# A@V on 64x32 tiles of TensorE in place of 64x64, in a fused attention and MLP kernel

## The chip, the cores and the metric

The kernel runs on one NeuronCore of a Trainium2 chip. The core has five engines that work side by side, each through its own list of instructions in order: TensorE (PE in the profile; its weight loads are listed apart as PEld), VectorE (DVE), ScalarE (ACT), GpSimd (POOL) and SyncE (SP). They wait for each other through semaphores. TensorE multiplies a stationary operand (the weights, loaded first) with a moving operand that is streamed through, and writes to PSUM, a memory of eight banks; VectorE and ScalarE read PSUM. The metric is the time in microseconds (us) from launch to end on the device.

TensorE's array of 128 rows by 128 columns can be used as smaller tiles. A matmul that contracts over 64 rows and gives 64 output features takes a tile of 64x64, and four of them fit side by side; one with 32 output features takes a tile of 64x32, and eight fit. Which tile a matmul uses follows from the partitions at which its operands and its output begin. Matmuls on different tiles can run at the same time.

## The reference

```python
def _attn_ref(q, k, v):                      # q, k, v: 8 x 12 x 448 x 64, float32
    scores = scale * np.matmul(q, k.transpose(0, 1, 3, 2))
    attn = np.maximum(scores, 0.0) ** 2 / S
    return np.matmul(attn, v)

x = attn_out.transpose(0, 2, 1, 3).reshape(B * S, H * D)     # 3584 x 768
h = x @ w_in                                                 # 768 x 2048
g = np.maximum(h, 0.0) + alpha * np.minimum(h, 0.0)
out = g @ w_out                                              # 2048 x 768
```

There is no softmax: the scores go through a ReLU and are squared. "A@V" below is the product of these squares with v.

## The kernel before

The 96 heads (8 batches of 12) are taken in 24 quads of four heads, three quads a batch. Within a quad, a head is addressed by r (which half of the 128 partitions holds its 64 features of q and k, or its 64 keys) and s or c (which 64 of 128 output partitions it fills). The 448 positions of a head are cut into NJ = 7 parts of 64.

Scores. `chunk` takes the next of 24 x 7 parts: `score_mm` multiplies the 64 keys of part j with all 448 queries, for four heads, into a pair of PSUM banks (one bank per r), and `relu` takes the pair out to `rl` on ScalarE (L237) or VectorE (L239). `square` makes `at` from it (L248 or L250). For quads 0 to 4 (`n <= PE_TURNED`) q and k were turned by TensorE, and a chunk is four matmuls on 64x64 tiles (L221). For quads 5 to 23 they were turned by VectorE's 32x32 transposes and DMAs (`turn_dma`, L202 and L208). There the keys of a part lie in two blocks of 32, so a chunk is eight matmuls of 32 keys on 64x32 tiles (L229), all with 448 moving columns.

A@V. `attnv(n)` multiplies, for one quad, the seven `at` tiles with v. For each part j there are four matmuls (r and s), each with 64 keys to contract, 64 features of v as the weights and the 448 queries as the moving operand. They accumulate over j in one pair of banks, r choosing the bank and s the half of the partitions. Then the pair is scaled and copied to `xT`, one bank by ScalarE (L272) and one by VectorE (L274), or both by one of them.

The MLP. `f1_mm` (L294) computes h from `xT` on the full 128x128 array, six matmuls a part; `f1_out` makes g (`gT`) with one ScalarE (L300) and one VectorE (L301) instruction. The output product is computed for blocks of 128 rows, either directly (`f2`, L319) or for pairs of blocks with seven half-size products in place of eight (`Pair`: TensorE L354, sums on VectorE L350 and L359, copies on ScalarE L370 and L375), with weights mixed beforehand (`weight_mix`, L332). These too use the full array.

Order. Nothing is scheduled by a tool: `tc.manual_schedule()` is on, and the plan strings passed to `walk` spell out the order of all work, word by word: `cADA` is three (here A, D, A) chunks with the engine of their ReLU, `s0D` a square, `v` an A@V, `f` one part of the first MLP product, `p..` and `r..` products of a pair, `g..` a direct block, `n` the turning of the next quad with the loads that follow it. Each engine executes its instructions in that order, so an instruction that waits holds up all that is behind it on its engine. An A@V is mostly placed between chunks of a later quad. PSUM banks are handed out least recently used first (`take_pair` for chunks and A@V, `take_bank` for the MLP), and a matmul into a bank waits until what was in it has been read.

The lines that matter here: L260 (A@V's matmul), L229 and L221 (scores), L294, L319 and L354 (MLP), and, as what TensorE waits for, L237, L239, L272, L274, L321, L359 and L375.

Of the kernel before, what the change touches and what calls it, by code (L numbers as in the profile page):

```python
# [16 lines left out]
NJ = 7  # L17
PE_TURNED = 4
# [3 lines left out]
def kernel(  # L22
# [10 lines left out]
    nc = tc.nc  # L33
    B, H, S, D = q.shape
# [46 lines left out]
    def take_pair():  # L81
        lo = min((0, 2, 4, 6), key=lambda i: (max(taken[i], taken[i + 1]), i))
        take(lo, 2)
        return psum[:, lo:lo + 2]
# [168 lines left out]
    def attnv(n, eng="AD"):  # L253
        ps = take_pair()
        vv = vraw.pop(n)
        for j in range(NJ):
            a = att.pop((n, j))
            for r in range(2):
                for s in range(2):
                    nc.tensor.matmul(ps[64 * s:64 * s + 64, r, :S],  # L260
                                     vv[64 * r:64 * r + 64, s, j, :],
                                     a[64 * r:64 * r + 64, s],
                                     start=(j == 0), stop=(j == NJ - 1))
        b, g = divmod(n, NG)
        if g == 0:
            xT[b] = xT_pool.tile([128, NG, 2, S], BF16, tag="xT", name="xT")
        if eng == "A":
            nc.scalar.activation(xT[b][:, g], ps[:, :, :S], ACTF.Copy, scale=out_scale)
            return
        for r in range(2):  # L270
            if eng[r] == "A":
                nc.scalar.activation(xT[b][:, g, r], ps[:, r, :S], ACTF.Copy, scale=out_scale)  # L272
            else:
                nc.vector.tensor_scalar(xT[b][:, g, r], ps[:, r, :S], out_scale, None, ALU.mult)  # L274
# [164 lines left out]
    class Walk:  # L439
# [12 lines left out]
        def step(self, w):  # L452
# [6 lines left out]
            elif c == "v":  # L459
                if turn["v"] < NQ:  # L460
                    attnv(turn["v"], rest or "AD")
                    turn["v"] += 1
# [108 lines left out]
```

## Time and profile before

| | |
|---|---|
| median of 3 runs | 395.19 us (394.13 to 396.29) |
| profiled execution | 394.87 us, of which the span of instructions is 393.1 us |
| granted TensorE clock, mean | 0.991 |
| TensorE busy | 372.5 us, 95% of the span, 3633 matmuls in the records |
| A@V matmuls (L260) | 672 (24 quads x 28), 36.6 us busy |
| scores on 64x32 tiles (L229) | 1064 (19 quads x 56), 38.0 us busy |
| scores on 64x64 tiles (L221) | 140 (5 quads x 28) |
| VectorE, ScalarE busy | 304.9 us (78%), 258.8 us (66%) |

A line of a group names the source line, the engine, the operation, the tiles it writes and reads, for matmuls the rows and columns of the array that it uses (64*32), the moving operand's shape and the number of instructions. A matmul's duration goes from its start to its modelled end; since the next matmuls start well before that end, what a run of matmuls costs is read from its start to the start of what follows. In a listing in order of time the first number is the start, counted from the start of the span, and the second the length. What stands in square brackets is the idle time of the engine before it, with what ended it.

### The profile page before, as it was taken

What the parts mean: (1) busy time and instruction counts of PE and PEld (TensorE: products, weight loads), DVE (VectorE), ACT (ScalarE), POOL (GpSimd) and SP (SyncE); (2) the same over time, 40 slices, a digit from 0 to 9 for tenths busy, and PEclk for the clock granted to TensorE, in tenths of its full rate; (3) what the DMA queues carried; (4) which work ended last, traced back from release to release, by engine and by line L of the source; (5) the groups of instructions that cost most, each with busy time, mean ns of one, the idle gap of its engine ahead of it and who ended that gap; (6) DMA issues with size and microseconds to landing.
All of it is one profiled execution on the core that took longest, in us unless ns stands there. A gap on an engine that the chain in (4) does not pass through costs nothing.

```text
span 393.1 us, 9204 instructions
## 1 busy us (share of the span) xinstructions
PE 372.5 (95%) x3633; PEld 195.9 (50%) x3637; DVE 304.9 (78%) x467; ACT 258.8 (66%) x384; POOL 86.4 (22%) x140
## 2 busy tenths in 40 slices
PE   8899999499989998999989999899999999999996
PEld 6454555144444454545545455445555555555563
DVE  4988988655996989867788886888969875865753
ACT  5987674456766656768668676786587785874400
POOL 8566563500330323011220311303000000000000
PEclk9999999889999999999999999999999999999999
DMA  9999999952677755726766257664333321220024
GB/s 148 191 203 202 207 209 206 223 109 47 100 147 152 117 95 79 166 42 116 136 109 140 43 97 141 108 144 66 76 62 81 76 49 26 64 65 9 2 51 110
DMA packets 51676, 43.38 MB, mean 110 GB/s; under 512 B 8753, under 2 KB 51121, under 8 KB 51633
## 3 DMA queue, kind: packets, MB, share of 16 engines
q0 software_dynamic: 27744, 22.59, 40.0%
q1 hardware_dynamic: 23216, 19.62, 19.6%
q8 instruction: 28, 0.46, 0.5%
q10 hardware_dynamic: 672, 0.59, 0.4%
q14 instruction: 16, 0.12, 0.1%
HBM read 45.62 MB, written 11.01 MB: 144 GB/s over the span
## 4 chain that ended last, share of the span: by engine, by line
PE 72%; DVE 12%; SPq 6%; DMA 4%; issue 3%; ACT 1%; DVEq 0%; ACTq 0%
PE psum L294 30%; PE psum L354 24%; PE psum L260 7%; PE psum L229 6%; SPq L208 5%; DVE perm L202 3%; DVE at L250 3%; DMA T<-perm 2%; PE psum L319 2%; DVE gT L301 2%; DMA T<-w_mix 1%; DVE S L350 1%; PE psum L171 1%; DVE rl L239 1%; PE psum L221 1%
## 5 line engine op out<-in xcount | busy, mean ns | idle before, releaser
L294 PE MATMUL psum<-xT,w_in_sb 128*128 128x448 bf16 x768 | 152.6, 356 | 0.4 <-DVE gT L301 0.4
L237 ACT ACTIVATE rl<-psum 128x896 bf16<-128x896 f32 x128 | 111.4, 929 | 25.9 <-PE psum L229 23.4
L301 DVE SCALAR_TENSOR_TENSOR gT<-neg,beta_sb,psum 128x448 bf16<-128x448 f32 x128 | 84.0, 675 | 36.1 <-ACT neg L300 34.9
L294 PEld LDWEIGHTS <-w_in_sb 128*128 128x128 bf16 x768 | 74.2, 99 | 75.0 <-issue 9.7
L300 ACT ACTIVATE neg<-psum 128x448 f32<-128x448 f32 x128 | 68.9, 546 | 55.3 <-PE psum L294 39.6
L250 DVE TENSOR_TENSOR at<-rl 128x896 bf16<-128x896 bf16 x105 | 62.1, 617 | 3.8 <-ACT rl L237 3.7
L248 ACT ACTIVATE at<-rl 128x896 bf16<-128x896 bf16 x63 | 58.3, 951 | 1.5 <-DVE rl L239 1.2
L123 POOL DMA_DIRECT2D qraw<-in_q_dram x38 | 22.6, 600 | 137.3 <-DVE perm L202 129.8
L354 PEld LDWEIGHTS <-S 128*128 128x128 bf16 x384 | 36.4, 98 | 32.7 <-issue 10.0
L239 DVE TENSOR_SCALAR rl<-psum 128x896 bf16<-128x896 f32 x40 | 43.2, 1086 | 9.3 <-PE psum L229 8.1
L354 PE MATMUL psum<-w_mix,S 128*128 128x384 bf16 x288 | 49.9, 326 | 0.0
L229 PE MATMUL psum<-T 64*32 64x448 bf16 x1064 | 38.0, 358 | 7.1 <-DMA T<-perm 5.4
L354 PEld LDWEIGHTS <-gT 128*128 128x128 bf16 x296 | 28.3, 98 | 20.2 <-issue 1.8
L260 PE MATMUL psum<-at,vraw 64*64 64x448 bf16 x672 | 36.6, 352 | 0.0
L354 PE MATMUL psum<-w_out_sb,gT 128*128 128x384 bf16 x192 | 34.0, 326 | 0.0
L130 POOL DMA_DIRECT2D vraw<-in_v_dram x24 | 17.7, 739 | 51.7 <-PE psum L260 49.7
L229 PEld LDWEIGHTS <-T 64*32 64x32 bf16 x1064 | 12.7, 90 | 29.3 <-issue 26.9
L260 PEld LDWEIGHTS <-vraw 64*64 64x64 bf16 x672 | 19.4, 106 | 14.7 <-issue 6.5
L359 DVE TENSOR_TENSOR osb<-psum,u 128x384 f32<-128x384 f32 (+2 forms) x37 | 19.7, 542 | 9.0 <-PE psum L354 8.4
L123 POOL DMA_DIRECT2D kraw<-in_k_dram x38 | 22.9, 614 | 3.3 <-DMA vraw<-in_v_dram 1.4
L319 PE MATMUL psum<-w_out_sb,gT 128*128 128x256 bf16 (+1 forms) x124 | 22.5, 325 | 0.9 <-DVE gT L301 0.5
L274 DVE TENSOR_SCALAR xT<-psum 128x448 bf16<-128x448 f32 x24 | 14.9, 623 | 10.0 <-PE psum L260 9.9
(46 smaller groups left out, 240.2 us busy)
## 6 DMA issues: line engine op xcount, KB each, us to landing
out_dram<-osb SPq DMA_DIRECT2D x91, 96.0 KB, 2.2
T<-perm SPq DMA_DIRECT2D x128, 56.0 KB, 3.6
vraw<-in_v_dram POOLq DMA_DIRECT2D x24, 224.0 KB, 6.1
qraw<-in_q_dram POOLq DMA_DIRECT2D x38, 112.0 KB, 3.3
kraw<-in_k_dram POOLq DMA_DIRECT2D x38, 112.0 KB, 4.7
w_in_sb<-in_moe_w_in_dram POOLq DMA_DIRECT2D x16, 192.0 KB, 8.2
w_out_sb<-in_moe_w_out_dram POOLq DMA_DIRECT2D x4, 512.0 KB, 10.4
T<-w_mix SPq DMA_DIRECT2D x24, 56.0 KB, 5.3
```

The source lines that it names most:

```text
L123: nc.gpsimd.dma_start(out=t[64 * m:64 * m + 64].rearrange("p w j d -> p w (j d)"), in_=flat[2 * g + m])
L229: nc.tensor.matmul(ps[lo:lo + 32, r, :S], t[64 * r:64 * r + 64, 1, a, NJ * c + j], moving, start=True, stop=True)
L237: nc.scalar.activation(rl, ps[:, :, :S], ACTF.Relu)
L239: nc.vector.tensor_scalar(rl, ps[:, :, :S], 0.0, None, ALU.max)
L248: nc.scalar.activation(a, rl, ACTF.Square)
L250: nc.vector.tensor_tensor(a, rl, rl, ALU.mult)
L260: nc.tensor.matmul(ps[64 * s:64 * s + 64, r, :S], vv[64 * r:64 * r + 64, s, j, :], a[64 * r:64 * r + 64, s], start=(j == 0), stop=(j == NJ ...
L294: nc.tensor.matmul(ps, w_in_sb[:, km // 2, km % 2, bass.ts(ff, 128)], xT[b][:, km // 2, km % 2, :], start=(km == 0), stop=(km == KM - 1))
L300: nc.scalar.activation(neg, ps, ACTF.Relu, scale=-1.0)
L301: nc.vector.scalar_tensor_tensor(gT[:, ff, (b % 2) * S:(b % 2) * S + S], neg, beta_sb[:, ff:ff + 1], ps, ALU.mult, ALU.add)
L319: nc.tensor.matmul(ps, gT[:, ff, bass.ts(c, 128)], w_out_sb[:, ff, first_col + lo:first_col + hi], start=(ff == 0), stop=(ff == KF - 1))
L354: nc.tensor.matmul(ps, left[:, i], right[:, i], start=(start and i == 0), stop=(i == KH - 1), skip_group_check=not start)
```

## The change

In `attnv`, the features of v are taken in slices of `width`: 64 for quads 0 to 3, as before, and 32 for quads 4 to 23. There each matmul with its weight load is replaced by two that stand one after the other. Each contracts the same 64 keys, streams the same 448 columns, has 32 features of v as its weights and writes 32 partitions of the bank. The order of the loops over j, r and s, the banks, the evacuations and all other work are as they were. The 560 matmuls of these 20 quads become 1120.

```diff
     def attnv(n, eng="AD"):
         ps = take_pair()
         vv = vraw.pop(n)
+        width = 64 if n < PE_TURNED else 32
         for j in range(NJ):
             a = att.pop((n, j))
             for r in range(2):
                 for s in range(2):
-                    nc.tensor.matmul(ps[64 * s:64 * s + 64, r, :S],
-                                     vv[64 * r:64 * r + 64, s, j, :],
-                                     a[64 * r:64 * r + 64, s],
-                                     start=(j == 0), stop=(j == NJ - 1))
+                    for lo in range(0, D, width):
+                        nc.tensor.matmul(ps[64 * s + lo:64 * s + lo + width, r, :S],
+                                         vv[64 * r:64 * r + 64, s, j, lo:lo + width],
+                                         a[64 * r:64 * r + 64, s],
+                                         start=(j == 0), stop=(j == NJ - 1))
```

## The prediction

> **What bounds the kernel now.** I read the profile's page first (busy shares, the chain that ended last, the costly groups), then the order in time of TensorE's matmuls around one A@V, then all engines there.
>
> ```profile
> PE 372.5 (95%) x3633; PEld 195.9 (50%) x3637; DVE 304.9 (78%) x467; ACT 258.8 (66%) x384; POOL 86.4 (22%) x140
> ...
> PE 72%; DVE 12%; SPq 6%; DMA 4%; issue 3%; ACT 1%; DVEq 0%; ACTq 0%
> PE psum L294 30%; PE psum L354 24%; PE psum L260 7%; PE psum L229 6%; SPq L208 5%; DVE perm L202 3%; DVE at L250 3%; DMA T<-perm 2%; PE psum L319 2%; DVE gT L301 2%; DMA T<-w_mix 1%; DVE S L350 1%; PE psum L171 1%; DVE rl L239 1%; PE psum L221 1%
> ...
> L229 PE MATMUL psum<-T 64*32 64x448 bf16 x1064 | 38.0, 358 | 7.1 <-DMA T<-perm 5.4
> L260 PE MATMUL psum<-at,vraw 64*64 64x448 bf16 x672 | 36.6, 352 | 0.0
> ```
>
> TensorE (PE) is busy 95% of the span and carries 72% of the chain; A@V (L260) is 7% of it and the scores (L229) 6%. So a change of A@V's time on TensorE reaches the end, wherever no other engine releases the next matmul. The mean of 352 ns is not A@V's price, because matmuls overlap; that is read from when one run of matmuls starts and when the next one does. TensorE in order of time (start, length, then the group):
>
> ```profile
> 192.96 0.38 PE L229 MATMUL psum<-T 64*32 64x448 bf16 x8
> 193.27 1.52 PE L260 MATMUL psum<-at,vraw 64*64 64x448 bf16 x28
> 194.72 0.57 PE L229 MATMUL psum<-T 64*32 64x448 bf16 x16
> 195.22 2.77 PE L354 MATMUL psum<-w_mix,S 128*128 128x384 bf16 x16
> ```
>
> From start to start: eight score matmuls take 0.31 us, sixteen 0.50, and 24 (206.10 to 206.79, below) 0.69. Each eight adds 0.19, and a run costs 0.12 besides. A@V takes 1.45 for seven groups of four: 7 x 0.19 + 0.12. So four matmuls on 64x64 tiles and eight on 64x32 tiles take the same 0.19, and every run of either shape pays 0.12 once. The next rows are from a place where A@V (quad 3) and the scores around it all use 64x64:
>
> ```profile
> 47.26 0.76 PE L221 MATMUL psum<-T 64*64 64x448 bf16 x12
> 47.85 1.49 PE L260 MATMUL psum<-at,vraw 64*64 64x448 bf16 x28
> 49.18 0.55 PE L221 MATMUL psum<-T 64*64 64x448 bf16 x8
> 49.66 0.61 PE L319 MATMUL psum<-w_out_sb,gT 128*128 128x256 bf16 x4
> ```
>
> Here the twelve take 0.59 (3 x 0.19 + 0.02) and A@V takes 1.33 (7 x 0.19). The 0.12 is gone, although operands and PSUM banks change as they do elsewhere. It is the price of a change of tile shape.
>
> **The change part by part.** Removed: 560 matmuls of 64 features with their weight loads. Added: 1120 of 32 features with theirs, so TensorE gets 1120 more instructions (7276 rows in the program become 8396). No other engine gets or loses an instruction, no DMA or wait is added or moved, and nothing passes another queue.
>
> The stream itself: 7 groups x 20 quads = 140 groups. Before, a group is four matmuls in 0.19 us; after, eight. The nearest row is the scores' eight on the same 64x32 tiles with the same 448 columns: 0.19. I take 0.19, so 0 us. Two things are not in any row: more than three such groups in succession (24 is the longest run, 48 instructions), and accumulation on 64x32 tiles (the scores only overwrite). Bounds: below, 0, since no row moves 448 columns faster than 0.19. Above, the densest longer stream of small matmuls, the 28 transposes at 25.45 to 26.36 us: 0.91 / 28 = 0.0325 us for a matmul and its load. Eight of these are 0.26, which is 0.07 more a group and 9.8 us over 140 groups.
>
> Here a rule speaks against the change. TensorE: Matmul & The Clock Gate, Part 1, section "Wait — 56ns, not 53.3ns?", says that starts of matmuls never come closer than about 25 ns on the average, however small they are. By it eight would need 0.20 us, 140 groups would lose 1.4 us, and the sum further down would shrink to a gain of some 0.5 us. The scores' rows above, 0.19 for eight or 24 ns each, lie just at or below this floor, so I go by the rows.
>
> The change of shape: an A@V between scores paid it on entry (the scores' run before it was 0.12 longer) and on leaving (its own run). Of the 20 quads, sixteen have scores on both sides, quad 10 only behind it (128x128 matmuls ahead), quad 18 only ahead, quads 5 and 23 neither. That makes 34 changes of shape that vanish, 34 x 0.12 = 4.1 us of TensorE's time. On borders to 128x128 matmuls the change of shape stays.
>
> How much of it reaches the end? Where TensorE then waits for an evacuation, it gains nothing. All engines around quad 13:
>
> ```profile
> 203.93 0.76 PE L229 MATMUL psum<-T 64*32 64x448 bf16 x24
> 204.03 0.56 DVE L359 TENSOR_TENSOR osb<-psum,u 128x384 f32<-128x384 f32 x1 [0.49 <-PE psum L354]
> 204.65 1.52 PE L260 MATMUL psum<-at,vraw 64*64 64x448 bf16 x28
> 206.10 0.76 PE L229 MATMUL psum<-T 64*32 64x448 bf16 x24
> 206.20 0.54 ACT L272 ACTIVATE xT<-psum 128x448 bf16<-128x448 f32 x1
> 206.79 4.07 PE L354 MATMUL psum<-w_mix,S 128*128 128x384 bf16 x24
> ```
>
> A@V starts 0.06 us after VectorE's L359 ends at 204.59: it needs the bank that L359 empties, so an earlier end of the scores' run is of no use. Behind it L354 starts 0.05 after ScalarE's xT copy ends at 206.74, and that copy starts when A@V ends; three groups of scores that finish sooner only wait for it. Going through the 26 borders of quads 9 to 23 in this way, twelve are tied like these or nearly so (quad 9's entry has 0.11 us): the entries of quads 9, 13, 16, 19, 20 and 22 and the far sides of 9, 10, 13, 16, 20 and 22. They count 0 (bounds 0 and 0.12 each, 1.4 together). Fourteen are free, entries of 11, 12, 14, 15, 17, 18, 21 and far sides of 11, 12, 14, 15, 17, 19, 21, with the other engines done 0.19 us or more before: 14 x 0.12 = 1.7 us. Of the eight borders of quads 4 to 8, quad 4's two lie on the chain with TensorE's own work behind them: 0.24. The others lead into the stretch from 97 to 133 us, where VectorE is busy 32.5 of 36 us and the chain runs over it and the transfers of T: 0 (at most 6 x 0.12 = 0.7).
>
> Sum: 1.7 + 0.24 = 1.9 us less. Cover used: the 560 further weight loads run beside matmuls (PEld is busy 50%); without that cover they would be part of the 0.26 above. Late next are the evacuations at the tied places, and VectorE in the pair stages: before its L359 at 196.74 it is idle for just 0.22 us.
>
> The profiled execution took 394.87 us (span 393.1 and 1.8 around it), 0.3 below the median of 395.19. Less 1.9 it would take 393.0; on the median's level 393.2.
>
> **The rivals.**
> A: slower. TensorE's queue can't be fed with sixteen instructions every 0.19 us through ten to thirteen groups in a row. For it: no run now holds more than 48 such instructions, and the transposes' row. Against it: the third group of a run follows as fast as the second, and 24 + 28 + 24 matmuls with loads (203.93 to 206.79) pass without a gap that VectorE does not explain. It decides from 1.9 / 140 = 0.014 us a group: at 0.204 the gain is gone, at 0.26 the time is 393.2 + 9.8 = 403.
> B: all the 4.1 us arrive, because the tied evacuations are themselves released by earlier TensorE work and move with it: 391.1. Against it stand the copies with 0.05 us to spare.
> C: the gain is swallowed. Between 264 and 286 us the chain goes over SyncE's transfers of T (from 270.08) and VectorE's perm and gT. Should these not start sooner, the free borders of quads 11 to 17, ten of them, are lost: 1.9 - 1.2 = 0.7 us of gain, 394.5. Against it: in the chain a piece of TensorE's L294 stands right before 270.08.
> D: the shape is not what costs 0.12, and nothing moves: 395.2. The rows of quad 3 speak against it.
>
> **How the numbers follow.** My forecast (gain 1.0 to 3.0 us, 392.2 to 394.2) 0.60; B (gain over 3.0) 0.12; C and D together 0.15; A 0.13. The range leaves out most of A and what is beyond B: 391.0 to 396.0. Half a per cent, about what a measurement of this kernel can tell from no change, is 2.0 us: faster than 393.2 are somewhat over half of the forecast and all of B, 0.44; within it the rest of the forecast, C, D and a little of A, 0.45; slower than 397.2 most of A, 0.11.
>
> **What would show it.** After, a run of 64x32 matmuls with A@V inside should take 0.19 us for each eight plus 0.12 once: at quad 12 from the scores' start to L354 10 x 0.19 + 0.12 = 2.0 in place of 2.26. A@V's 56 matmuls should take 1.33 from start to start between scores and 1.45 beside 128x128 matmuls. If a group takes 0.20 or more, A is right. If the runs are short and the span is not, C: then the idle time of TensorE before L354 and at 264 to 286 us has grown. The tied places should show TensorE starting L354 0.05 us after the xT copy still. The prediction is wrong if the feeding of TensorE fails, or if the tied places move with the rest.

## The result and the profile after

The changed kernel takes 391.17 us (median of 13 runs, 390.07 to 393.30) and the kernel before, measured beside it, 394.24 (13 runs, 393.48 to 396.29). The ratio is 0.9919 with a 95% interval of 0.9899 to 0.9939, so 3.1 us less (2.4 to 4.0). The forecast was 1.9 us less (1.0 to 3.0, 392.2 to 394.2 us), with 391.0 to 396.0 as the range.

From the page of the changed kernel (busy time of the engines; then A@V's group with its two shapes added up; then the queue that brings instructions, which the page of before gives as 28 packets and 0.46 MB):

```profile
PE 368.0 (94%) x4193; PEld 197.3 (51%) x4197; DVE 305.0 (78%) x467; ACT 258.4 (66%) x384; POOL 86.4 (22%) x140
...
L262 PE MATMUL psum<-at,vraw 64*32 64x448 bf16 (+1 forms) x1232 | 37.2, 350 | 0.0
...
q8 instruction: 33, 0.54, 0.6%
```

560 matmuls more, and TensorE is busy 4.5 us less. VectorE and ScalarE work as long as before. Lines below the edit have moved by two: L260 is now L262, L294 is L296, L354 is L356, L272 is L274, L359 is L361. The text goes on calling the first MLP product's runs L294.

TensorE in order of time around quad 12, the free place of the prediction:

```profile
190.77 0.38 PE L229 MATMUL psum<-T 64*32 64x448 bf16 x8
190.97 1.51 PE L262 MATMUL psum<-at,vraw 64*32 64x448 bf16 x56
192.29 0.56 PE L229 MATMUL psum<-T 64*32 64x448 bf16 x16
192.79 2.77 PE L356 MATMUL psum<-w_mix,S 128*128 128x384 bf16 x16
```

The eight score matmuls take 0.20 us from start to start (before 0.31), A@V 1.32 (1.45), and the whole run 2.02 in place of 2.26. That is 10 x 0.19 + 0.12. Ten groups of eight follow each other at 0.19 each; in the kernel before there were never more than three in a row.

All engines around quad 13, the tied place:

```profile
201.49 0.76 PE L229 MATMUL psum<-T 64*32 64x448 bf16 x24
201.59 0.56 DVE L361 TENSOR_TENSOR osb<-psum,u 128x384 f32<-128x384 f32 x1 [0.49 <-PE psum L356]
202.21 1.52 PE L262 MATMUL psum<-at,vraw 64*32 64x448 bf16 x56
203.53 0.76 PE L229 MATMUL psum<-T 64*32 64x448 bf16 x24
203.76 0.54 ACT L274 ACTIVATE xT<-psum 128x448 bf16<-128x448 f32 x1
204.35 1.95 PE L356 MATMUL psum<-w_mix,S 128*128 128x384 bf16 x11
```

A@V again starts 0.06 us after L361 ends at 202.15, and L356 0.05 after the xT copy ends at 204.30. Between them A@V to the scores is 1.32 and not 1.45, but the scores to L356 are 0.82 and not 0.69. From 201.49 to 204.35 it is 2.86 us, as before (203.93 to 206.79). The run got shorter and the wait behind it longer by the same 0.13.

Where the 3.7 us between the two profiled spans (393.1 and 389.4) came from, by the starts of the same runs in the two traces: 1.80 between the L294 run at 133.33 us and the last one at 352.62 (131.45 and 348.94 after), 0.26 between 96.64 and 131.34, and 1.74 between 61.86 and 86.58, where TensorE waits for the transfers of T. The first 61.86 us give nothing (0.11 longer). TensorE in this last stretch, before:

```profile
61.86 8.50 PE L294 MATMUL psum<-xT,w_in_sb 128*128 128x448 bf16 x44
73.25 0.37 PE L229 MATMUL psum<-T 64*32 64x448 bf16 x4 [2.90 <-DMA T<-perm]
76.12 1.31 PE L229 MATMUL psum<-T 64*32 64x448 bf16 x20 [2.50 <-DMA T<-perm]
77.36 9.29 PE L294 MATMUL psum<-xT,w_in_sb 128*128 128x448 bf16 x36
86.58 0.76 PE L229 MATMUL psum<-T 64*32 64x448 bf16 x24
```

and after:

```profile
61.97 8.50 PE L296 MATMUL psum<-xT,w_in_sb 128*128 128x448 bf16 x44
72.14 0.37 PE L229 MATMUL psum<-T 64*32 64x448 bf16 x4 [1.67 <-DMA T<-perm]
75.34 1.31 PE L229 MATMUL psum<-T 64*32 64x448 bf16 x20 [2.83 <-DVE gT L303]
76.58 8.44 PE L296 MATMUL psum<-xT,w_in_sb 128*128 128x448 bf16 x36
84.95 0.76 PE L229 MATMUL psum<-T 64*32 64x448 bf16 x24
```

The view puts the second wait after down to VectorE's gT, which had ended just then. In both traces that wait ends 0.24 us after the last of the eight transfers of T has landed.

### The profile page after: what moved, and what is told of

Same layout as the page of the kernel before. It is cut to its first block, busy times and chain, and to the rows that moved or that the text cites. A ratio compares the mean times of both kernels' runs of the same rounds, so it can differ in the third digit from the quotient of the medians.

```text
span 389.4 us, 10324 instructions
## 1 busy us (share of the span) xinstructions
PE 368.0 (94%) x4193; PEld 197.3 (51%) x4197; DVE 305.0 (78%) x467; ACT 258.4 (66%) x384; POOL 86.4 (22%) x140
## 4 chain that ended last, share of the span: by engine, by line
PE 57%; DVE 7%; ACT 2%; issue 2%; DMA 1%; DVEq 0%; SPq 0%; ACTq 0%
PE psum L296 24%; PE psum L356 23%; PE psum L262 5%; PE psum L229 4%; DVE perm L202 2%; DVE at L250 1%; DVE gT L303 1%; PE psum L321 1%; DMA out_dram<-osb 1%; ACT neg L302 1%; DVE S L352 1%; DVE osb L361 1%; ACT xT L274 1%; DVE rl L239 1%; DMA T<-perm 1%
## 5 line engine op out<-in xcount | busy, mean ns | idle before, releaser
L296 PE MATMUL psum<-xT,w_in_sb 128*128 128x448 bf16 x768 | 151.7, 355 | 0.4 <-DVE gT L303 0.4
L237 ACT ACTIVATE rl<-psum 128x896 bf16<-128x896 f32 x128 | 111.3, 922 | 24.5 <-PE psum L229 22.2
L296 PEld LDWEIGHTS <-w_in_sb 128*128 128x128 bf16 x768 | 73.9, 98 | 74.4 <-issue 8.7
L356 PEld LDWEIGHTS <-S 128*128 128x128 bf16 x384 | 36.7, 98 | 32.9 <-issue 10.0
L239 DVE TENSOR_SCALAR rl<-psum 128x896 bf16<-128x896 f32 x40 | 43.2, 1086 | 9.3 <-PE psum L229 8.2
L356 PE MATMUL psum<-w_mix,S 128*128 128x384 bf16 x288 | 49.8, 326 | 0.2
L356 PEld LDWEIGHTS <-gT 128*128 128x128 bf16 x296 | 28.3, 98 | 20.2 <-issue 1.8
L262 PE MATMUL psum<-at,vraw 64*32 64x448 bf16 (+1 forms) x1232 | 37.2, 350 | 0.0
L356 PE MATMUL psum<-w_out_sb,gT 128*128 128x384 bf16 x192 | 34.0, 326 | 0.0
L229 PEld LDWEIGHTS <-T 64*32 64x32 bf16 x1064 | 14.5, 91 | 25.6 <-issue 21.0
L262 PEld LDWEIGHTS <-vraw 64*32 64x32 bf16 (+1 forms) x1232 | 20.4, 93 | 13.0 <-issue 3.5
L361 DVE TENSOR_TENSOR osb<-psum,u 128x384 f32<-128x384 f32 (+2 forms) x37 | 19.8, 543 | 9.0 <-PE psum L356 8.4
```

Of the source, the lines that this page charges most:

```text
L229: nc.tensor.matmul(ps[lo:lo + 32, r, :S], t[64 * r:64 * r + 64, 1, a, NJ * c + j], moving, start=True, stop=True)
L237: nc.scalar.activation(rl, ps[:, :, :S], ACTF.Relu)
L239: nc.vector.tensor_scalar(rl, ps[:, :, :S], 0.0, None, ALU.max)
L262: nc.tensor.matmul(ps[64 * s + lo:64 * s + lo + width, r, :S], vv[64 * r:64 * r + 64, s, j, lo:lo + width], a[64 * r:64 * r + 64, s], star ...
L296: nc.tensor.matmul(ps, w_in_sb[:, km // 2, km % 2, bass.ts(ff, 128)], xT[b][:, km // 2, km % 2, :], start=(km == 0), stop=(km == KM - 1))
L356: nc.tensor.matmul(ps, left[:, i], right[:, i], start=(start and i == 0), stop=(i == KH - 1), skip_group_check=not start)
```

## The experiments

Each edit is against the changed kernel, whose line is `width = 64 if n < PE_TURNED else 32`. The expectations call the theory of the record "theory", keep its rival B, and name two more. E: most of the gain is made in the first 90 us, by transfers of T that land earlier. F: 64x32 tiles or small weight loads are faster in themselves, whatever the neighbours' shape. "Steps" below are differences in start times of the same runs of matmuls between two traces.

**Free borders alone.**

```diff
+        width = 32 if n in (11, 12, 14, 15, 17, 21) else 64
```

> 32 features only in quads 11, 12, 14, 15, 17 and 21, whose twelve borders with scores are free: nothing that TensorE waits for ends there less than 0.19 us before. Theory (a vanished change of shape gives about 0.12 us on TensorE, and it reaches the end only at free borders): each of the twelve steps shows in the trace, 12 x 0.12 = 1.4 us less than before, ratio about 0.9964. Rival B (tied borders pay as well, so the free ones are not special): by number of borders 12 of 34 of the measured 3.1 us, 1.1 us less, ratio 0.9972, with the rest to be found in the tied quads. Rival E (most of the gain is made in the first 90 us, by transfers of T that land earlier): hardly anything from these quads, at most 0.5 us, ratio over 0.9987.

Measured: 392.10 against 394.56 us, ratio 0.994 (0.9917 to 0.9963). In the trace, every one of the twelve borders shows a step of 0.11 to 0.13, and from 132.77 to 350.61 us, the starts of the same two L294 runs as above, it is 217.84 us in place of 219.29: 1.45 less. The steps are as theory has them; the time fell by 2.4 us (1.5 to 3.3), a microsecond more than the steps, which the interval only just reaches. Nothing here explains that microsecond.

**Tied borders alone.**

```diff
+        width = 32 if n in (9, 10, 13, 16, 20, 22) else 64
```

> 32 features only in quads 9, 10, 13, 16, 20 and 22, whose eleven borders with scores are tied to an evacuation that ends 0.05 to 0.11 us before TensorE goes on. Theory: runs of matmuls get shorter by 0.1 to 0.13 us each and TensorE waits that much longer right behind, so the time is that of before, ratio 0.9995 to 1.0005. Rival B (the evacuations move with TensorE): up to 11 x 0.12 = 1.3 us less, ratio 0.9967. Rival E: as before.

Measured: 394.04 against 394.56 us, ratio 0.9985 (0.9968 to 1.0002). At quads 10, 13, 16, 20 and 22 the trace shows a step of -0.11 to -0.13 behind the A@V, and one of +0.12 to +0.13 at the matmul behind the next scores; quad 9 gains 0.11 and 0.12 and loses 0.12 and 0.06 behind. Of all the steps together 0.09 is left (219.20 in place of 219.29). Rival B falls by these steps; the ratio by itself says less, since its interval ends right beside B's 0.9967. On one chip, the six free quads are 1.9 us faster than the six tied ones.

**A change of shape put back inside A@V.**

```diff
-        width = 64 if n < PE_TURNED else 32
         for j in range(NJ):
             a = att.pop((n, j))
+            width = 32 if n >= PE_TURNED and j != 3 else 64
```

> As the changed kernel, but the fourth of the seven groups of an A@V (j = 3) goes back to four matmuls on 64x64 tiles, in quads 4 to 23. The work on the array is the same, there are 80 matmuls fewer, and each A@V gets two changes of shape inside. Theory (the change of shape costs about 0.12 us): an A@V between scores goes from 1.32 back to some 1.55 us from start to start, 20 x 0.24 = 4.8 us more than the changed kernel if all were on the path, and 3.6 from the fifteen quads 9 to 23 that are; ratio to before 1.000 to 1.004. Rival F (64x32 tiles or the smaller weight loads are what gains): six of seven groups still have them, so 6/7 of the gain stays, ratio about 0.993.

Measured: 395.71 against 394.56 us, ratio 1.0036 (1.002 to 1.0052). It is slower than the kernel before, though six of seven groups have 64x32 tiles. TensorE around quad 12 in this kernel:

```profile
191.39 0.38 PE L229 MATMUL psum<-T 64*32 64x448 bf16 x8
191.59 1.75 PE L262 MATMUL psum<-at,vraw 64*32 64x448 bf16 x52
193.16 0.56 PE L229 MATMUL psum<-T 64*32 64x448 bf16 x16
```

A@V takes 1.57 from start to start: 1.33 and twice 0.12. Of the two L294 runs, the second starts 221.28 us after the first, 3.8 more than in the changed kernel and 2.0 more than in the kernel before. F falls: with two changes of shape back in each A@V the gain is gone, and each step goes with a change of shape.

**All 24 quads.**

```diff
+        width = 32
```

> 32 features in all 24 quads. The scores of quads 0 to 4 stay on 64x64 tiles, so A@V of quads 0, 1 and 3, which now has the shape of its neighbours, gets two changes of shape each, and quad 2 (128x64 transposes behind it, 128x128 ahead) stays as it is. Theory (the change of shape is what costs): quad 3's A@V goes from 1.33 to 1.45 us from start to start and the scores ahead of it from 0.59 to 0.69, and quads 0 and 1 likewise; up to 6 x 0.12 = 0.7 us more than the changed kernel where TensorE is on the path, so ratio to before between 0.992 and 0.994. Rival F (64x32 tiles are themselves faster, and the shape of the neighbours does not matter): the four quads gain as the others did, 4/20 of 3.1 = 0.6 us less than the changed kernel, ratio about 0.9905.

Measured: 391.79 against 394.56 us, ratio 0.9929 (0.9901 to 0.9957). By time it can't be told from the changed kernel. In order of time, quad 3 with its neighbours still on 64x64 tiles:

```profile
47.80 0.76 PE L221 MATMUL psum<-T 64*64 64x448 bf16 x12
48.50 1.52 PE L262 MATMUL psum<-at,vraw 64*32 64x448 bf16 x56
49.94 0.57 PE L221 MATMUL psum<-T 64*64 64x448 bf16 x8
50.45 0.72 PE L321 MATMUL psum<-w_out_sb,gT 128*128 128x256 bf16 x5
```

The twelve take 0.70 in place of 0.59 and A@V 1.44 in place of 1.33. The same 64x32 tiles that gain from quad 4 on lose here, since here they differ from their neighbours.

**Quads 4 to 8 alone, in two sets.**

```diff
+        width = 32 if 4 <= n < 9 else 64
```

> 32 features only in quads 4 to 8. Theory: 0.24 us from quad 4 at most, and VectorE, the transfers of T and the evacuations take back most of the rest, so 0 to 0.5 us less than before, ratio 0.9987 to 1.0000. Rival E (the transfers of T that TensorE waits for at 70 to 76 us land 1.2 to 1.6 us earlier because of the change): 1.2 to 1.6 us less, ratio 0.996 to 0.997, with that wait short in the trace.

> 32 features only in quads 4 to 8, once more. Open is whether the changed kernel's lead over before is 2.0 us (1.8 from quads 9 to 23, 0.24 from quad 8) or about 3, with the rest made between 62 and 87 us, where TensorE waits for the transfers of T and then runs at half the clock for 3.4 or 6.8 us. Over that stretch, six profiles without 32 features in quads 4 to 8 stand at -1.2 us on the average from the first profile of before (0 to -2.5), seven with them at -2.1 (-1.3 to -2.9). If the difference of 0.8 is the change's, this run is 1.0 us faster than before, ratio 0.9974. If it is the scatter between executions, only quad 8's 0.24 is left, ratio 0.9994.

Measured: 393.04 against 393.90 us, ratio 0.9986 (0.9971 to 1.0002), and 392.62 against 393.80, ratio 0.9969 (0.9954 to 0.9985). The first alone decides nothing; the two together stand near 0.9978, 0.9 us less, by an estimate from their intervals 0.4 to 1.3. Both traces show -0.24 to -0.25 between 96.64 and 131.34 (quad 8's two borders; quad 6's is lost again at quad 7). That leaves some 0.65 of the 0.9, which the traces put between 62 and 87 us.

**The same kernels again.** The kernel before and the changed one, unedited, for more profiles:

> The kernel before, for a second profile of it. The question is the wait of TensorE for the transfers of T at 70 to 76 us: 5.4 us in the first profile of before and 1.7 with the wait for VectorE at 2.8 in the changed kernel's. If it varies by a microsecond or more between executions of one kernel, that part of the difference between the two traces is not the change's. If it is again 5.4 with loads issued at the same times to 0.1 us, rival E is kept.

> The changed kernel, for a second profile of it. Behind 131 us the steps between it and any profile of before should be the same to 0.02 us at each border (1.8 us in all). In the first 90 us theory expects a difference of some tenths to a microsecond from its own first profile, since the loads come in another order in each execution; rival E expects the same 1.9 us lead over before there.

Measured: 395.89 and 390.15 us. From 131 us on, the lead of this second changed profile is 1.79 us over the first profile of before and 1.86 over the second. Ahead of that, two executions of one kernel differ by up to 2.5 us, mostly within the first 12.

**Before, late half and changed kernel on one chip.** The unedited kernel before; 32 features in quads 9 to 23 only; the unedited changed kernel:

```diff
+        width = 32 if n >= 9 else 64
```

> The kernel before, timed against itself, to see how far two groups of runs of one kernel on one chip come apart. Both theories expect a ratio of 1.000 with an interval of about 0.002 to either side; how far its median lies from the other's is the error that every comparison of this set carries.

> 32 features only in quads 9 to 23, nothing changed in the first 131 us. Theory: the steps behind 131 us are those of the changed kernel, 1.8 us in all, so 1.8 us less than before, ratio 0.9954, and the changed kernel is 0.2 to 0.3 us faster still (quad 8's two borders). Rival E (the first 90 us gain by the change): 1.2 us more than that are missing, so the changed kernel is 1.2 to 1.5 us faster than this one.

> The changed kernel once more, beside the one above and the one before on the same chip. Theory: 2.0 us less than before from the steps in the trace, ratio 0.9949, and 0.2 to 0.3 us less than with quads 9 to 23 alone. Rival E: 3.1 us less than before, ratio 0.992, and 1.2 to 1.5 us less than with quads 9 to 23 alone.

Measured against 394.17 us: the kernel before 0.9994 (0.9981 to 1.0006), quads 9 to 23 alone 0.9954 (0.9939 to 0.9969), the changed kernel 0.9920 (0.9900 to 0.9940). The middle one is what theory had for it, 1.8 us less. The last is 1.7 us below it in the medians (392.13 and 390.46) and 1.3 by the ratios, where theory had 0.2 to 0.3 and E 1.2 to 1.5. So something in the early part gains more than quad 8's borders.

**One run fewer.**

```diff
-... pb cADA v p1 cAAA s0A p6 ...
+... pb cADA v cAAA p1 s0A p6 ...
```

> The changed kernel with one more change of shape removed: behind quad 18's A@V the three chunks of scores come before the product p1 and not after it, so that seven chunks' worth of 64x32 matmuls stand as one run in place of two. Theory: one run fewer, 0.12 us less from that place on, if the reluctant part, the emptying of PSUM for the three chunks, keeps up (ReLUs of 0.9 to 1.1 us on two engines for six chunks in about 2.5 us); otherwise TensorE waits there and it comes out between 0 and 0.5 us slower. By the clock it is the same as the changed kernel to 0.1%.

Measured: 391.05 against 394.17 us, ratio 0.9929 (0.9914 to 0.9943), not told from the changed kernel by time. In its trace TensorE stops in the joined run:

```profile
283.14 1.51 PE L262 MATMUL psum<-at,vraw 64*32 64x448 bf16 x56
284.47 0.37 PE L229 MATMUL psum<-T 64*32 64x448 bf16 x8
285.28 0.73 PE L229 MATMUL psum<-T 64*32 64x448 bf16 x16 [0.44 <-DVE rl L239]
```

The second group of the joined scores needs the banks that VectorE's ReLU empties. From quad 18's scores to quad 19's it is 12.58 us in place of 12.10 in the changed kernel: 0.48 lost to save 0.12.

## Why the prediction was right or wrong

**The time: inside the range, partly by luck.** 391.17 us lies 0.2 above the lower end of the range and outside the 392.2 to 394.2 of the forecast itself. It is the time of rival B (391.1), whose mechanism did not come. Two things made up the difference from 393.2, about a microsecond each. The kernel before ran at 394.24 and not at the 395.19 of its first three runs. And the gain was 3.1 and not 1.9, for the reasons below.

**What a group costs: right.** Eight matmuls on 64x32 tiles took 0.19 us, accumulating or not, over ten groups in a row. The 0.26 of the transposes was far off as an upper bound, and rival A did not come. The Trainium skill's floor of 25 ns between starts (TensorE: Matmul & The Clock Gate, section "Wait — 56ns, not 53.3ns?") would have made it 0.20; the run of quad 12 has 2.02 us for 80 matmuls with the 0.12 in it, 24 ns each without. No run here is slowed by that floor, and in the records the starts of one group, on different tiles, are mostly 2 to 5 ns apart. One group of the 140 in the first trace did stop TensorE by 0.1 us without a wait that the trace shows (quad 5, whose A@V took 1.73 us in place of 1.45); in the seven other traces with 32 features in quads 4 to 8 there is no such stop.

**The change of shape at 0.12: right,** shown from both sides. Taking it away gave 0.11 to 0.13 a border at the free places, and putting two into each A@V cost 0.24 apiece.

**Fourteen free borders and twelve tied: right in the sum, at quad 19 by luck.** 1.7 us were forecast for quads 9 to 23, and 1.80 measured in the changed kernel, 1.82 with these quads alone. Rival B asked for the tied ones to move with the rest; they stayed, to 0.09 us. Rival C asked for the gains to be lost between 264 and 286 us; there the lead stays at 3.2 us. At quad 19 the forecast had the entry tied and the far side free. The entry gained 0.13 and A@V 0.16, and 0.18 was lost in the next scores: their first group starts in two halves 0.17 apart, and their second, which needs VectorE's ReLU (L239, done at 297.32 us), at 297.38. That makes 0.11 in all, where 0.12 had been counted. Rival D fell with the kernel that puts the shape change back.

**The term of quads 4 to 8: wrong in place and size.** The step that failed is "quad 4's two lie on the chain with TensorE's own work behind them: 0.24. The others lead into the stretch from 97 to 133 us ...: 0". Quad 4's lead is 0.26 us right behind it in the first trace and is cut to 0.11 at the next L294 run: the scores ahead of that take 0.66 us (55.85 to 56.51) in place of 0.50. No wait stands behind this. In the scores ahead of A@V, four matmuls had started at 53.20 and the next four, after a wait for T, at 54.12; from then on the two halves of a group start 0.16 apart, all the way to L294, where the last half is paid for. In the kernel before, A@V's other shape ended this. What is left of the lead is gone before or in the wait for T. Quad 8's two borders, counted 0, come through with 0.24: behind them TensorE goes on with L294, and the xT copies that it needs there are done 0.6 us before their matmuls in the kernel before, 0.5 in the changed one. That alone would have left the sum at 1.80 + 0.24 = 2.0.

**What the sum lacked: some 0.8 us between 62 and 87 us.** From the L294 run at 61.86 to the scores at 86.58 (the same two runs in each kernel), the six profiles without 32 features in quads 4 to 8 take 22.2 to 24.7 us, 23.5 on the average. The eight with them take 21.8 to 23.4, 22.7 on the average. So 1.74 between the two first profiles overstated it, because the first profile of before is the longest of its six; but a difference of 0.8 is left, and with it the sum is 2.8 against the measured 3.1 (2.4 to 4.0). From executions that scatter this much, the 0.8 has an interval of about -0.1 to 1.7. That it is more than scatter rests on the timings: quads 4 to 8 alone give 0.9, with quad 8's 0.24 in it, and the changed kernel is 1.3 to 1.7 faster than quads 9 to 23 alone. So rival E was right in part, at about half of its size.

Behind it stands a step that the prediction wrote off with "no DMA or wait is added or moved". TensorE's instructions are themselves fetched by DMA, 16 KB at a time (q8: 28 fetches before, 30 with 336 instructions more, 33 with 1120, 34 with 1344), and with more instructions the fetches fall elsewhere. SyncE's eight issues of T for quad 6 (number, shortest, median and longest in ns, first and last start), in the kernel before:

```profile
L208 SPq DMA_DIRECT2D T<-perm x8: 595/598/1429, 64.7 to 70.1; - x8
```

and with 32 features in quads 4 to 8 alone:

```profile
L208 SPq DMA_DIRECT2D T<-perm x8: 594/596/645, 64.4 to 69.0; - x8
```

In the kernel before the third issue took 1.43 us, not 0.6. The transfers in a window of 0.8 us around it, by queue:

```profile
q0 software_dynamic: 168, 0.15, 116.5%
q8 instruction: 1, 0.02, 7.6%
...
T<-perm SPq DMA_DIRECT2D x1, 56.0 KB, 6.6
```

A fetch of instructions for TensorE (q8) begins at 66.16 us, within 0.1 us of that issue. The same holds in all six profiles without the early change: a fetch begins 0.1 us after to 0.5 before the start of one issue of T, and that issue takes 0.83 to 1.43 us. In all eight profiles with it the fetch begins at 63.6 to 65.3 us, 0.3 to 1.1 us ahead of the first issue of T, and no issue but the first overlaps it (which takes 0.64 or 0.65 in all fourteen); the eight issues then take 5.2 us together, against 5.4 to 6.0. TensorE's wait for the second half of T ends on the average 0.5 us sooner after the first issue (10.2 us behind it in the eight, 10.75 in the six). The wait is followed by a stretch in which the granted clock is 0.5, of 6.8 us in five of the six and of 6.8 in five and 3.4 in three of the eight. The rest of the fourteen traces says the same of the fetch. L208 makes 2128 issues in them. Leaving out those that come first in a row, a fetch begins between 0.5 us before and 0.15 us after the start of 50, and 48 of these take 0.81 to 2.55 us; of the 1743 that overlap no fetch, 8 take over 0.75. So that a fetch lengthens an issue beside it is close to shown, though no run moved a fetch by itself. What it is worth is less sure: the eight issues take 0.4 us less on the average, and the wait ends 0.5 sooner. The other 0.3 of the 0.8 come behind the wait, where the stretch at half the clock was short in three traces of eight and in one of six, which may be chance. That part stays open.

## What to carry to other kernels

Runs of matmuls on smaller tiles cost a fixed 0.12 us each here, whatever their length, when the array changes tile shape at their borders. So adjacent runs should have one shape, even if it takes twice as many matmuls, as long as the groups on the array take the same time. Before such a saving is counted, look at each place for the evacuation that ends 0.05 us before the next matmul: there it only lengthens a wait. And two profiles can differ by microseconds where a kernel waits for transfers; a stretch is compared with several profiles of the kernel before.

## What was not expected of the hardware

Sixteen instructions for every 0.19 us did not slow TensorE, but for the one stop at quad 5. 5 more fetches of 16 KB (33 in place of 28) moved where these fetches fall, and the issue of T by SyncE that started close to one took 0.83 to 1.43 us in place of 0.6, while the first of the eight issues took 0.64 or 0.65 with a fetch beside it and without. This is not tied to full DMA engines, as they are between 54 and 82 us here: in the kernel before, the issue at 270.71 us, beside a fetch at 270.70, took 2.49 us, where the DMA engines were busy 47% of the time (265 to 275 us). So adding instructions to one engine can shift the time of another. And where a group's second half starts late, runs of one shape carry the shift of some 0.16 us on until the shape changes: at quad 4 the change to L294 paid for it.
